# Chunked attention and two feed-forward layers: the first layer's weights stored later as two halves, and SiLU as one ScalarE operation

## The chip, the cores and the metric

The kernel runs on one core of a Trainium2 chip. The metric is the device time of one execution in microseconds (us); where several runs are given, their median. Shorter is better.

## The reference, cut to what matters

Three stages run in a row, all in float32: attention in chunks of 32 queries with 8 memory keys, then two feed-forward layers (FFN) on 3072 tokens of width 512.

```python
attn = softmax(scale * q_c @ k_full.T) @ v_full      # 4 x 8 heads, 768 positions, head size 64
x = relu(attn_tokens @ w_in) ** 2 @ w_out            # first FFN,  512 -> 2048 -> 512
g, val = x @ w_gate, x @ w_val                       # second FFN, 512 -> 1536 -> 512
out = (g * sigmoid(g) * val) @ moe2_w_out
```

The product of g and sigmoid(g) is SiLU. All weights arrive as pairs of 32-bit words (64-bit floats), so each must be put together into float32 before use.

## The kernel before, in words

**Products.** TensorE multiplies in a rounded float32 form. For accuracy each operand is split into a rounded part hi and a rest lo, and a product is three matmuls: lo by hi, hi by lo, hi by hi (`TERMS`, line 41). `split` (line 440) makes the two parts: an ACT copy writes hi, and a subtraction on DVE or POOL writes lo.

**Stages.** The 3072 tokens are six blocks of 512. Attention is 24 units, four to a block. Four units run ahead of all else; the others run beside the matmuls of blocks one to four (numbered j = 0 to 3 in the code). Blocks one to four go through the first FFN directly: for each of 16 groups i of 128 hidden columns, `first_layer` (line 698) is 12 matmuls, `hidden` (713) squares the ReLU and splits it, and `first_out` (728) is 12 matmuls. The second FFN then runs over three pairs of blocks with a product of two-by-two blocks in seven multiplications instead of eight; for the last pair the first FFN goes that way too. In such a pair `quads` (934) computes the hidden columns, `out_layer` (1040) the output, and `second_quads` (1006) gives the element work between the products. The seven-way product needs sums and differences of weight blocks, the left sides. `sides` (758) forms one set of them from two inputs, splits each, and stores it to DRAM through the buffers of pool G4; `Left.load_in` (818) and `Left.load_out` (845) fetch them again.

**Weights.** `words` (382) loads 512 KB of word pairs into a buffer of pool G4, and with two ACT and four DVE operations makes a 128x512 float32 tile `a` in pool G2. `prep1` (685) does this for the 32 pieces of the first FFN (16 of w_in, 16 of w_out) during block one (j = 0): it calls `words`, **stores `a` to DRAM** (lines 689 to 692, tensors `w1d`, shown as win and wout in the trace), and splits `a` into the tile that the matmuls read (`w1b`, 1024 wide: hi, then lo). That tile stays in SBUF until block four is done. Much later the 16 sets of left sides of the first FFN (`left1`, lines 1216 to 1225) read the stored `a` back: `whole_of` (858) loads one 128x512 tile in one part (w_in, 256 KB) or two (w_out, 128 KB each), 48 loads in all, 8.4 MB. The 18 sets of the second FFN (`left2`, lines 1212 to 1215) use `words` instead.

**SiLU.** `third` and `second` in `second_quads` (lines 1015 to 1023) add the last product of g, write sigmoid(g) with ACT into another tile, and multiply that tile by g with `sub` (459) on DVE or POOL, whichever the planner takes. There are two such multiplications for each of 12 groups and three pairs, 72 in all.

**Order.** Nothing is scheduled by hand: `Plan` (86) lists every operation with an assumed cost for each engine that may do it, ranks it by when TensorE needs it, and plays the program through on paper, one event after another. The result is a fixed order for each engine. On the chip each engine, and the DMA queue of SP through which all transfers are issued, takes its instructions in that order and waits at each until its inputs are there. A pool has as many buffers as `sizes` (line 328) says: G4 three and G2 six, and two and four more after the tile of block three's tokens (pool X1) is given up. Each set of left sides has a due time in the plan, taken from `SIDES` (line 305): (start, spacing, number) for the two groups, left2 and left1.

```python
def whole_of(parts):
    ...
            pl.op(
                {"SP": 0.08},
                lambda key=key, src=src, o=o, wide=wide: nc.sync.dma_start(
                    out=at(a)[:, o : o + wide], in_=w1d[key][:, src : src + wide]
                ),
                (w1k[key], token), ((a, n),), move=rate(512 * wide),
            )
```

Of the kernel before, what the change touches and what calls it, by code (L numbers as in the profile page):

```python
# [9 lines left out]
F32 = mybir.dt.float32  # L10
# [3 lines left out]
AF = mybir.ActivationFunctionType  # L14
ALU = mybir.AluOpType
AX = mybir.AxisListType

P = 128
# [8 lines left out]
NF1, NF2 = DFF1 // P, DFF2 // P  # L27
# [274 lines left out]

STAGED = 14.5
FIRST = -9.0
SIDES = ((150.0, 20.5, NF2 + NF2 // 2), (540.0, 18.0, NF1))

BY_PE = tuple(range(8))

# [1 line left out]
C512 = {"ACT": 0.63}  # L310
EITHER = {"ACT": 0.63, "DVE": 0.72}
DIFF = {"DVE": 0.69, "POOL": 1.3}
# [3 lines left out]
def rate(nbytes):  # L316
    return nbytes / 370e3
# [3 lines left out]
def tile_chunked_attention_two_ffn(ctx: ExitStack, tc, qd, kd, vd, w1, w2, wo2, out):  # L321
    nc = tc.nc
    pl = Plan()
# [6 lines left out]
    dr = ctx.enter_context(tc.tile_pool(name="dr", bufs=1, space=bass.MemoryType.DRAM))  # L330
# [35 lines left out]
    def home(b):  # L366
        if b.pool in BEYOND and b.slot >= sizes[b.pool]:
            name, first = BEYOND[b.pool]
            return name, b.slot - sizes[b.pool] + first
        return b.pool, b.slot  # L370

    def at(b):
        name, n = home(b)
        return homes[name][n]

    def external(name):
        return pl.buf(None, name)

    xb = external("x")
# [60 lines left out]
    def split(dst, src, reads, keys, n=512, diff=None):  # L440

        k = n / 512
        pl.op(
            {"ACT": 0.2 + 0.43 * k},
            lambda: nc.scalar.activation(out=dst(HI), in_=src(), func=AF.Copy),  # L445
            reads, [(b, (q, HI)) for b, q in keys],
        )
        costs = {"DVE": 0.16 + 0.56 * k, "POOL": 0.25 + 1.1 * k} if diff is None else diff

        def low(e):  # L450
            eng = nc.gpsimd if e == "POOL" else nc.vector
            eng.tensor_tensor(out=dst(LO), in0=src(), in1=dst(HI).bitcast(F32), op=ALU.subtract)  # L452

        pl.op(
            costs, low, list(reads) + [(b, (q, HI)) for b, q in keys], [(b, (q, LO)) for b, q in keys],
            shared=diff is not FROM,
        )

    def sub(out, x, y, op=ALU.subtract, engs=None):


        def run(e):
            eng = nc.gpsimd if e == "POOL" else nc.vector
            eng.tensor_tensor(out=out[1](), in0=x[1](), in1=y[1](), op=op)  # L464

        return pl.op(engs or DIFF, run, (x[0], y[0]), (out[0],), shared=engs is not FROM)

    def copy(out, x, engs=None, func=AF.Copy):
        def run(e):
            if e == "DVE":  # L470
                nc.vector.tensor_copy(out[1](), x[1]())
            else:
                nc.scalar.activation(out=out[1](), in_=x[1](), func=func)  # L473

        return pl.op(engs or {"ACT": 0.6}, run, (x[0],), (out[0],))

    def whole(b):
        return (b, lambda: at(b))
# [198 lines left out]
    def unit(u, pool="A4"):  # L677
        return Unit(u, pool, pool == "S0")


    w1b = {}
    w1d = {(k, i): dr.tile([P, 512], F32, name=f"w{k}{i}") for k in ("in", "out") for i in range(NF1)}
    w1k = {k: external("w") for k in w1d}

    def prep1(kind, i):
        a = words(w1[i, :, 1024 * (kind == "out") :][:, 0:1024])
        b = pl.buf("W1" if kind == "out" and i >= 4 else "R", "w1")
        w1b[kind, i] = b
        pl.op(
            {"SP": 0.08}, lambda: nc.sync.dma_start(out=w1d[kind, i], in_=at(a)),  # L690
            (a,), (w1k[kind, i],), move=rate(262144),
        )
        split(
            lambda h: at(b)[:, 512 * h : 512 * h + 512], lambda: at(a), (a,), ((b, 0),),
            diff={"DVE": 0.72, "POOL": 1.35},
        )

    def first_layer(i, xb):
        hp, w = pl.buf("PS", "hp"), w1b["in", i]

        def run():
            x = at(xb).rearrange("p (h k t) -> p h k t", h=2, k=KC)
            terms = [(a, b, k) for a, b in TERMS for k in range(KC)]
            for n, (a, b, k) in enumerate(terms):
                nc.tensor.matmul(  # L705
                    at(hp), at(w)[:, 512 * a + k * P : 512 * a + (k + 1) * P], x[:, b, k, :],
                    start=(n == 0), stop=(n == len(terms) - 1),
                )

        pl.op({"PE": 2.75}, run, (xb, w), (hp,), tail=0.2)  # L710
        return hp

    def hidden(hp):
# [41 lines left out]

    due = [a + n * d for a, d, k in SIDES for n in range(k)]

# [100 lines left out]
    def whole_of(parts):  # L858


        def make(token):
            a, o = pl.buf("G2", "a"), 0
            for n, (key, src, wide) in enumerate(parts):
                pl.op(
                    {"SP": 0.08},
                    lambda key=key, src=src, o=o, wide=wide: nc.sync.dma_start(
                        out=at(a)[:, o : o + wide], in_=w1d[key][:, src : src + wide]
                    ),
                    (w1k[key], token), ((a, n),), move=rate(512 * wide),
                )  # L870
                o += wide
            return a

        return make
# [131 lines left out]
    def second_quads(left, r):  # L1006

        got = []

        def begin(n):  # L1010
            a, d, e, f = (pl.buf("T2", x) for x in "adef")
            b, c = pl.buf("U", "b"), pl.buf("U", "c")
            got.append((b, c))

            def third(k):
                sub(whole(e), whole(e), whole(k), ALU.add, FROM)
                copy(whole(f), whole(e), func=AF.Sigmoid, engs=C512)
                sub(whole(f), whole(f), whole(e), ALU.mult)

            def second(k):  # L1020
                sub(whole(a), whole(a), whole(k), ALU.add, FROM)
                copy(whole(d), whole(a), func=AF.Sigmoid, engs=C512)
                sub(whole(d), whole(d), whole(a), ALU.mult)

            def seventh(k):
                sub(whole(c), whole(k), whole(c), ALU.add, FROM)
                sub(whole(c), whole(c), whole(f), ALU.mult)

            return {
                1: lambda k: copy(whole(a), whole(k)),  # L1030
                5: lambda k: copy(whole(c), whole(k)),
                6: lambda k: copy(whole(e), whole(k)),
                3: third, 2: second, 7: seventh,
                4: lambda k: sub(whole(b), whole(k), whole(d), ALU.mult, FROM),
            }

        quads([lambda q=q: left.load_in(q) for q in range(NF2)], r, begin)
        return got
# [65 lines left out]
    def put_out(p):  # L1104
        def put(x, row, col):
# [16 lines left out]
            out=ident, in_=ident, pattern=[[-1, P]], compare_op=ALU.is_equal, fill=0.0,  # L1122
# [6 lines left out]
    xs = {0: pl.buf("X1", "x")}  # L1129
# [44 lines left out]
    for j in range(DIRECT):  # L1174
        if j + 1 < DIRECT:
            xs[j + 1] = pl.buf(("X", "X1")[j % 2], "x")
        for i in range(NF1):
            if j == 0:
                for kind, n in at_slot.get(i, ()):
                    pl.due = FIRST if i == 0 else None  # L1180
                    prep1(kind, n)
                    pl.due = None
                if i == NF1 - 1:
                    for s in (NF1, NF1 + 1):
                        for kind, n in at_slot.get(s, ()):
                            prep1(kind, n)
            for what in "MTLAB":
                for op, u in todo.get((j, i), ()):
                    if op != what:
                        continue  # L1190
                    if op == "A":
                        units[u] = unit(u)
                        units[u].scores()
                    elif op == "B":
                        units[u].weigh()
                    elif op == "T":
                        units[u].turn_pe() if u in BY_PE else units[u].turn()
                    elif op == "M":
                        units[u].mix()
                    elif op == "L":  # L1200
                        if u // 4 < DIRECT:
                            units[u].leave(xs[u // 4], u % 4)
                        else:
                            units[u].leave_far(u // 4 - DIRECT, u % 4)
            hp = first_layer(i, xs[j])
            pend.append((j, i, hidden(hp)))
            if len(pend) > LAG:
                flush()
# [18 lines left out]
    src, token = (*yd[:-1], xd), (*yb[:-1], xb)  # L1227
# [112 lines left out]
```

## Time and profile before

| | |
|---|---|
| median of 3 runs | 1145.23 us (1144.47 to 1146.02) |
| the profiled execution: own time, span | 1146.57 us, 1144.9 us |
| TensorE (PE) busy | 1101.8 us, 96% of the span |
| VectorE (DVE) busy | 901.6 us, 79% |
| ScalarE (ACT) busy | 609.2 us, 53% |
| GpSimd (POOL) busy | 242.2 us, 21% |
| moved by DMA | 305.24 MB, mean 267 GB/s |
| chain that ended last | PE 72%, DVE 11%, DMA 8%, issue 5%, ACT 4%, POOL 1% |

In the trace a tile is named by its pool without its number: g and gg are tiles of G4, f and ff of G2, t of T2, u and a of U, r and x hold operands for TensorE, ps is PSUM. `tma` and `tmb` are left2's sides in DRAM (for the hidden layer and the output), `tla` and `tlb` those of left1. A line can be that of a helper: 452 is the lo part of `split`, 464 the body of `sub`, 473 that of `copy`, 425, 433, 410 and 417 the DVE operations of `words`. "SPq" is the queue in which SP issues transfers. An arrow `<-` in a wait points at what the engine waited for.

The stretches of the span, read off where the lines change: attention ahead of block one to 30 us; block one to about 135; blocks two to four to about 468, with left2's sides beside them; the first pair's hidden layer to 576 and its output to 645; the second pair's to 758 and 824; the first FFN of the last pair to 965; the last pair's second FFN from there to the end.

### The profile page before, as it was taken

What the parts mean: (1) busy time and instruction counts of PE and PEld (TensorE: products, weight loads), DVE (VectorE), ACT (ScalarE), POOL (GpSimd) and SP (SyncE); (2) the same over time, 40 slices, a digit from 0 to 9 for tenths busy, and PEclk for the clock granted to TensorE, in tenths of its full rate; (3) what the DMA queues carried; (4) which work ended last, traced back from release to release, by engine and by line L of the source; (5) the groups of instructions that cost most, each with busy time, mean ns of one, the idle gap of its engine ahead of it and who ended that gap; (6) DMA issues with size and microseconds to landing.
All of it is one profiled execution on the core that took longest, in us unless ns stands there. A gap on an engine that the chain in (4) does not pass through costs nothing.

```text
span 1144.9 us, 17301 instructions
## 1 busy us (share of the span) xinstructions
PE 1101.8 (96%) x6044; PEld 893.9 (78%) x6044; DVE 901.6 (79%) x1573; ACT 609.2 (53%) x1071; POOL 242.2 (21%) x202
## 2 busy tenths in 40 slices
PE   5898999999999999999899999999999999999998
PEld 5676788888888887788687788878888887888786
DVE  6989898869888998789998967898847963645981
ACT  3878764455546566455564444565536642433560
POOL 2211000012121342212944511334500100000100
PEclk9999999999999999999999999999999999999999
DMA  8877855566756877999689999989984677755552
GB/s 340 303 250 260 267 188 179 170 232 227 263 192 243 293 267 282 399 345 357 205 307 360 365 415 371 361 275 335 352 333 148 202 228 275 259 193 175 178 179 94
DMA packets 111591, 305.24 MB, mean 267 GB/s; under 512 B 12048, under 2 KB 20240, under 8 KB 111504
## 3 DMA queue, kind: packets, MB, share of 16 engines
q1 hardware_dynamic: 111504, 304.14, 75.3%
q8 instruction: 48, 0.79, 0.3%
q14 instruction: 39, 0.32, 0.1%
HBM read 218.63 MB, written 85.46 MB: 266 GB/s over the span
## 4 chain that ended last, share of the span: by engine, by line
PE 72%; DVE 11%; DMA 8%; issue 5%; ACT 4%; POOL 1%; SPq 0%; ACTq 0%; DVEq 0%; POOLq 0%
PE ps L926 30%; PE ps L1063 17%; PE ps L705 11%; PE ps L733 10%; DMA g<-in_w 4%; DVE r L452 2%; PE ps L519 2%; PE ps L646 2%; DVE f L425 1%; ACT r L445 1%; DVE t L464 1%; DMA tla<-g 1%; DVE u L464 1%; DMA s<-in_k 1%; DMA r<-tmb 1%
## 5 line engine op out<-in xcount | busy, mean ns | idle before, releaser
L926 PE MATMUL ps<-r,r 128*128 128x512 f32 x1314 | 317.2, 391 | 8.6 <-DVE u L464 5.2
L926 PEld LDWEIGHTS ps<-r,r 128*128 128x128 f32 x1314 | 246.1, 188 | 65.4 <-DVE u L464 6.8
L473 ACT ACTIVATE t<-ps 128x512 f32<-128x512 f32 x171 | 100.9, 595 | 208.1 <-PE ps L926 92.5
L1063 PE MATMUL ps<-r,r 128*128 128x512 f32 x816 | 192.9, 389 | 1.6 <-ACT r L445 1.3
L1063 PEld LDWEIGHTS ps<-r,r 128*128 128x128 f32 x816 | 153.0, 188 | 34.3 <-ACT r L445 1.7
L733 PE MATMUL ps<-r,w 128*128 128x512 f32 x576 | 141.5, 395 | 7.1 <-DVE w L452 6.4
L733 PEld LDWEIGHTS ps<-r,w 128*128 128x128 f32 x576 | 107.4, 188 | 33.3 <-DVE w L452 8.6
L452 DVE TENSOR_TENSOR r<-u,r 128x512 fp32r<-128x512 f32 x138 | 101.3, 755 | 33.5 <-ACT r L445 27.2
L445 ACT ACTIVATE r<-u 128x512 fp32r<-128x512 f32 x149 | 89.0, 625 | 65.3 <-PE ps L1063 29.3
L705 PE MATMUL ps<-xx,r 128*128 128x512 f32 x384 | 98.2, 405 | 5.0 <-DVE r L452 4.7
L705 PE MATMUL ps<-x,r 128*128 128x512 f32 x384 | 94.3, 394 | 0.0
L705 PEld LDWEIGHTS ps<-xx,r 128*128 128x128 f32 x384 | 71.7, 190 | 23.8 <-DVE r L452 6.1
L926 PE MATMUL ps<-r,x 128*128 128x512 f32 x330 | 83.5, 395 | 1.9 <-ACT t L473 1.0
L464 DVE TENSOR_TENSOR t<-t,ps 128x512 f32<-128x512 f32 x72 | 49.0, 682 | 45.8 <-PE ps L926 40.1
L705 PEld LDWEIGHTS ps<-x,r 128*128 128x128 f32 x384 | 70.9, 188 | 15.4
L595 DVE STREAM_TRANSPOSE a<-t 32x128 f32<-32x128 f32 x256 | 77.4, 303 | 5.0 <-PE ps L646 0.9
L473 ACT ACTIVATE t<-t 128x512 f32<-128x512 f32 x72 | 45.3, 631 | 57.5 <-DVE t L464 55.9
L926 PEld LDWEIGHTS ps<-r,x 128*128 128x128 f32 x330 | 62.5, 190 | 16.6 <-DVE r L452 1.6
L452 POOL TENSOR_TENSOR r<-t,r 128x512 fp32r<-128x512 f32 x29 | 40.7, 1404 | 140.3 <-ACT r L445 114.3
L445 ACT ACTIVATE g<-f 128x512 fp32r<-128x512 f32 (+1 forms) x70 | 40.2, 576 | 35.8 <-POOL f L464 11.7
L464 POOL TENSOR_TENSOR u<-u,u 128x512 f32<-128x512 f32 x8 | 11.9, 1494 | 198.5 <-DVE r L452 196.0
L926 PE MATMUL ps<-x,r 128*128 128x512 f32 x180 | 51.4, 394 | 0.5 <-ACT t L473 0.5
(152 smaller groups left out, 1686.5 us busy)
## 6 DMA issues: line engine op xcount, KB each, us to landing
r<-tma SPq DMA_DIRECT2D x88, 512.0 KB, 6.3
r<-tmb SPq DMA_DIRECT2D x56, 512.0 KB, 5.5
g<-in_w SPq DMA_DIRECT2D x54, 512.0 KB, 5.1
tma<-g SPq DMA_DIRECT2D x29, 512.0 KB, 4.6
r<-tlb SPq DMA_DIRECT2D x24, 512.0 KB, 4.4
a<-in_q SPq DMA_DIRECT2D x20, 512.0 KB, 4.4
a<-in_k SPq DMA_DIRECT2D x20, 512.0 KB, 4.9
a<-in_v SPq DMA_DIRECT2D x20, 512.0 KB, 4.5
```

The costliest lines, as they stand in the source:

```text
L425: lambda: nc.vector.scalar_tensor_tensor(out=at(a).bitcast(I32), in0=word(1), scalar=-0x40000000, in1=at(a).bitcast(I32), op0=ALU.bitwise_ ...
L445: lambda: nc.scalar.activation(out=dst(HI), in_=src(), func=AF.Copy),
L452: eng.tensor_tensor(out=dst(LO), in0=src(), in1=dst(HI).bitcast(F32), op=ALU.subtract)
L464: eng.tensor_tensor(out=out[1](), in0=x[1](), in1=y[1](), op=op)
L473: nc.scalar.activation(out=out[1](), in_=x[1](), func=func)
L519: nc.tensor.matmul(o[64 * par : 64 * par + 64, s, f, m, :], q[:, s, m, ci, :], k[:, s, m, ci, :], start=True, stop=True,)
L595: nc.vector.transpose(out=o[g : g + 32, hh, :, :, m, :].rearrange("k s (f c) q -> k s f c q", c=2)[:, :, :, par, :], in_=a[r : r + 32, :, ...
L646: nc.tensor.matmul(o[64 * hh : 64 * hh + 64, 2 * s : 2 * s + 2, CH * ci : CH * ci + CH], a[:, hh, s, ci, :], b[:, hh, s, ci].rearrange("p ...
L705: nc.tensor.matmul(at(hp), at(w)[:, 512 * a + k * P : 512 * a + (k + 1) * P], x[:, b, k, :], start=(n == 0), stop=(n == len(terms) - 1),)
L733: nc.tensor.matmul(at(accs[m]), at(w)[:, 512 * a + m * P : 512 * a + (m + 1) * P], at(h2)[:, 512 * b : 512 * b + 512], start=(i == 0 and n ...
L926: nc.tensor.matmul(at(bank), at(w[slot])[:, o : o + P], at(r[i, n])[:, 512 * b : 512 * b + 512], start=(first and n == 0 and m == 0), stop ...
L1063: nc.tensor.matmul(at(bank[i][n]), at(w[i][g // 2])[:, o : o + P], at(r)[:, 512 * b : 512 * b + 512], start=(first and m == 0), stop=(g == ...
```

## The change

The 32 stores of `a` leave `prep1`. In their place `keep1` stores the finished tile, hi and lo, 512 KB for each piece: the 16 of w_in beside block two (j = 1), the 16 of w_out beside block three (j = 2). The name `begun` orders each store behind the matmuls of group i in the plan alone; no memory stands behind it. `whole_of` loads hi and lo into two tiles of G2 and adds them on DVE or POOL, so 48 loads become 96 and 32 additions come in. The multiplications behind the sigmoid go, and ACT writes SiLU itself. The due times of the left sides move.

```diff
-SIDES = ((150.0, 20.5, NF2 + NF2 // 2), (540.0, 18.0, NF1))
+SIDES = ((150.0, 22.0, NF2 + NF2 // 2), (560.0, 16.0, NF1))
...
-    w1d = {(k, i): dr.tile([P, 512], F32, name=f"w{k}{i}") for k in ("in", "out") for i in range(NF1)}
+    w1d = {(k, i): dr.tile([P, 1024], F32, name=f"w{k}{i}") for k in ("in", "out") for i in range(NF1)}
...
     def prep1(kind, i):
...
-        pl.op(
-            {"SP": 0.08}, lambda: nc.sync.dma_start(out=w1d[kind, i], in_=at(a)),
-            (a,), (w1k[kind, i],), move=rate(262144),
-        )
...
+    def keep1(kind, i, j):
+
+        b = w1b[kind, i]
+        pl.op(
+            {"SP": 0.08},
+            lambda: nc.sync.dma_start(out=w1d[kind, i], in_=at(b).bitcast(F32)),
+            (b, (begun, (j, i))), (w1k[kind, i],), move=rate(524288),
+        )
...
     def whole_of(parts):
...
+                for b, c in ((a, src), (t, 512 + src)):
+                    pl.op(
+                        {"SP": 0.08},
+                        lambda b=b, c=c, key=key, o=o, wide=wide: nc.sync.dma_start(
+                            out=at(b)[:, o : o + wide], in_=w1d[key][:, c : c + wide]
+                        ),
+                        (w1k[key], token), ((b, n),), move=rate(512 * wide),
+                    )
...
+            pl.op(
+                DIFF,
+                lambda e: (nc.gpsimd if e == "POOL" else nc.vector).tensor_tensor(
+                    out=at(a), in0=at(a), in1=at(t), op=ALU.add
+                ),
+                keys, keys[: len(parts)], shared=True,
+            )
...
             def third(k):
                 sub(whole(e), whole(e), whole(k), ALU.add, FROM)
-                copy(whole(f), whole(e), func=AF.Sigmoid, engs=C512)
-                sub(whole(f), whole(f), whole(e), ALU.mult)
+                copy(whole(f), whole(e), func=AF.Silu, engs=C512)
 
             def second(k):
                 sub(whole(a), whole(a), whole(k), ALU.add, FROM)
-                copy(whole(d), whole(a), func=AF.Sigmoid, engs=C512)
-                sub(whole(d), whole(d), whole(a), ALU.mult)
+                copy(whole(d), whole(a), func=AF.Silu, engs=C512)
...
+            hp = first_layer(j, i, xs[j])
+            if j in (1, 2):
+                keep1(("in", "out")[j - 1], i, j)
```

## Rows read from the trace of the kernel before

**Rows 1.** Windows by stage: us, busy (instructions) of PE, PEld, DVE, ACT, POOL; PEclk, DMA share, GB/s
```profile
30.00:135.00 105.00, 91.60 (x570) 70.36 (x569) 95.49 (x170) 81.95 (x145) 18.42 (x15) 0.98 0.81 271
135.00:400.00 265.00, 265.00 (x1954) 214.35 (x1953) 222.36 (x522) 143.26 (x250) 41.58 (x40) 1.00 0.65 223
...
468.00:545.00 77.00, 76.25 (x335) 62.90 (x336) 65.62 (x103) 40.78 (x72) 19.82 (x15) 1.00 0.97 360
545.00:576.00 31.00, 25.42 (x98) 19.75 (x98) 30.41 (x31) 15.87 (x30) 27.27 (x21) 0.89 0.65 224
576.00:645.00 69.00, 66.43 (x288) 53.52 (x287) 61.80 (x95) 39.93 (x74) 29.87 (x21) 1.00 0.92 331
645.00:758.00 113.00, 110.65 (x484) 90.33 (x484) 90.57 (x133) 57.24 (x104) 34.57 (x33) 1.00 1.01 379
758.00:824.00 66.00, 65.87 (x289) 53.92 (x289) 60.24 (x91) 36.41 (x68) 28.28 (x21) 1.00 0.91 316
```

**Rows 2.** Waits of PE in block one, 30 to 135 us: total us, times, longest
```profile
PE ps L733 <- DVE w L452: 6.4, 5, 1.5
PE ps L705 <- DVE r L452: 4.7, 5, 1.9
```

**Rows 3.** Waits of SP's queue in the same stretch: total us, times, longest
```profile
SPq L386 <- DVE f L425: 43.1, 25, 4.6
SPq L690 <- DVE f L417: 14.0, 13, 1.9
```

**Rows 4.** DMA issues, 30 to 135 us: count, KB each, median us to landing
```profile
g<-in_w SPq DMA_DIRECT2D x27, 512.0 KB, 5.3
```

**Rows 5.** DMA issues, 135 to 320 us
```profile
g<-in_w SPq DMA_DIRECT2D x14, 512.0 KB, 4.8
...
a<-in_q SPq DMA_DIRECT2D x11, 512.0 KB, 4.4
```

**Rows 6.** Waits of PE, 545 to 645 us
```profile
PE ps L926 <- DVE u L464: 4.6, 2, 3.4
```

**Rows 7.** Groups by line and shape, whole span: count, busy us, mean ns, idle before
```profile
L464 DVE TENSOR_TENSOR t<-t,t 128x512 f32<-128x512 f32 x61 | 46.4, 764 | 1.6 <-ACT t L473 1.6
...
L473 ACT ACTIVATE t<-t 128x512 f32<-128x512 f32 x72 | 45.3, 631 | 57.5 <-DVE t L464 55.9 <-DVE a L464 0.6
...
L464 POOL TENSOR_TENSOR t<-t,t 128x512 f32<-128x512 f32 x11 | 15.1, 1370 | 111.7 <-ACT t L473 111.6
```

**Rows 8.** The same view, ACT alone: the table load at the first sigmoid
```profile
L473 ACT ACT_TABLE_LOAD x1 | 1.3, 1283 | 0.0
```

**Rows 9.** Groups by line and shape, 440 to 580 us
```profile
L464 POOL TENSOR_TENSOR t<-t,t 128x512 f32<-128x512 f32 x10 | 13.8, 1377 | 63.6 <-ACT t L473 63.5
L464 DVE TENSOR_TENSOR t<-t,t 128x512 f32<-128x512 f32 x14 | 11.1, 799 | 0.0
```

**Rows 10.** Timeline of DVE, 541 to 548 us: start, us, operation
```profile
541.56 0.68 DVE L452 TENSOR_TENSOR gg<-ff,gg 128x512 fp32r<-128x512 f32 x1
542.16 1.78 DVE L464 TENSOR_TENSOR u<-u,t 128x512 f32<-128x512 f32 x1
```

**Rows 11.** Timeline of POOL, the same stretch
```profile
542.10 1.30 POOL L452 TENSOR_TENSOR r<-u,r 128x512 fp32r<-128x512 f32 x1 [3.29 <-ACT r L445]
```

**Rows 12.** Timeline, 525 to 600 us: the last word pairs of left2
```profile
537.67 0.42 SPq L386 DMA_DIRECT2D g<-in_wo  x1
```

**Rows 13.** Chain that ended last, at the ends of two hidden layers: start, us, what
```profile
744.23 2.01 DVE t L464 x2
...
1082.07 1.92 DVE t L464 x2
```

**Rows 14.** Windows of 50 us: the one with the most GB/s
```profile
650.00:700.00 50.00, 49.22 (x216) 40.09 (x215) 35.95 (x55) 22.72 (x40) 9.71 (x11) 1.00 1.03 404
```

**Rows 15.** DMA issues, 560 to 824 us
```profile
f<-wout SPq DMA_DIRECT2D x22, 128.0 KB, 5.9
f<-win SPq DMA_DIRECT2D x9, 256.0 KB, 7.1
```

More of the change, by code (lines that the diff above doesn't have):

```diff
@@ L696, in prep1, with first_layer @@
         )
-    def first_layer(i, xb):
+    def keep1(kind, i, j):
[5 more added lines that the diff above has]
+        )
+    begun = external("begun")
+    def first_layer(j, i, xb):
         hp, w = pl.buf("PS", "hp"), w1b["in", i]
@@ L708, in run @@
                 )
-        pl.op({"PE": 2.75}, run, (xb, w), (hp,), tail=0.2)
+        pl.op({"PE": 2.75}, run, (xb, w), (hp, (begun, (j, i))), tail=0.2)
         return hp
@@ L861, in make @@
         def make(token):
-            a, o = pl.buf("G2", "a"), 0
+            a, t, o = pl.buf("G2", "a"), pl.buf("G2", "t"), 0
             for n, (key, src, wide) in enumerate(parts):
[L864 to L870, printed above, removed]
-                o += wide
+                for b, c in ((a, src), (t, 512 + src)):
[6 more added lines that the diff above has]
+                    )
+                o += wide
+            keys = [(b, n) for b in (a, t) for n in range(len(parts))]
+            pl.op(
[5 more added lines that the diff above has]
+            )
             return a
@@ L1204, in tile_chunked_attention_two_ffn @@
                             units[u].leave_far(u // 4 - DIRECT, u % 4)
-            hp = first_layer(i, xs[j])
+            hp = first_layer(j, i, xs[j])
+            if j in (1, 2):
+                keep1(("in", "out")[j - 1], i, j)
             pend.append((j, i, hidden(hp)))
```

## The prediction

> **What bounds the kernel now.** I read the windows by stage first, for where TensorE (PE) is not busy. In blocks two to four it never stops: 265.00 of 265 us, at full granted clock [rows 1]. Nothing that the change does there can gain, and it costs nothing as long as that cover stands. Time is lost in two places. In block one PE is busy 91.60 of 105 us, so 13.4 us are idle. At the end of the first pair's hidden layer it is busy 25.42 of 31 us, and the mean granted clock is 0.89 of full there [rows 1]: 5.6 us idle, and 0.11 x 31 = 3.4 us to the lower clock. The output layer behind it is short of 2.6 us, and the second pair's hidden layer of 2.4 us. Ahead of block one lies attention, and the change has no part in it.
>
> Then the waits, for whose fault it is. In block one PE waits for the lo parts of weights (6.4 us) and of hidden tiles (4.7 us), both DVE's [rows 2]. DVE is busy 95.49 of 105 us [rows 1]. The queue of SP shows the other half of the loop: the loads of word pairs wait 43.1 us, in 25 waits, for line 425, the last operation that reads a G4 buffer [rows 3]. So block one is a ring of three buffers: load, two ACT and three DVE operations, next load. With 27 loads in 105 us [rows 4], one turn of a buffer takes 3 x 105 / 27 = 11.7 us, of which 5.3 us is the load's time to landing. Ring and DVE are nearly equal bounds.
>
> At 545 to 576 us PE waits for DVE's sums over tiles u (4.6 us) [rows 6], DVE is busy 30.41 and POOL 27.27 of 31 us [rows 1]. POOL is no free help: the same size of DVE operation takes 0.68 us alone and 1.78 us when it starts 0.06 us behind a POOL operation of 1.30 us [rows 10, 11].
>
> **The change, part by part.** The sum is made against the profiled execution's 1146.57 us (span 1144.9 us); the median shown is 1145.23, that is 1.34 us less, so I take the sum off the median in the end.
>
> *The 32 stores leave block one.* That is 8.4 MB fewer transfers in a stretch that moved 271 GB/s at a DMA share of 0.81; they also leave SP's queue, where they waited for DVE (14.0 us on line 417 alone) [rows 1, 3] with loads behind them. That wait cost little, since those loads had to wait for line 425 anyway. What the stores cost is landing time of the loads. Later, at a share of 0.65, the same loads land in 4.8 us and attention's loads of equal size in 4.4 [rows 1, 5]. So a turn shrinks by 0.5 to 0.9 us of 11.7: 4 to 8 us over 105. DVE caps it: with 95.49 us of work it can give back 9.5 us at most, and it becomes the next wait. I take 4 us, the low end, because DVE is already 91% busy. Bounds: 0 (DVE takes all of it) to 9.5.
>
> *Stores of hi and lo in blocks two and three.* 32 x 0.52 = 16.8 MB more, beside PE that never waits. On SP they are 32 issues at about 0.42 us [rows 12], an estimate of 13 us of queue time over 175 us; they wait for nothing, since hi and lo are long made. Behind them stand loads of word pairs for left2. If these land as in block one, 0.5 us later [rows 4, 5], left2's sides slip by some us; their last load was issued at 537.67 us [rows 12], the output layer that needs them begins at 576. I cost it at nothing. If that cover went, PE would wait at 576 for what is missing, at most a few us.
>
> *SiLU in ACT.* Each of the 72 ACT operations stays, at 631 ns [rows 7]; no row has a SiLU, so its price lies between that and 631 + 764 ns, as if ACT did both steps one after the other; I take 631, the row of the same operation on the same tiles, and ACT, idle for half of 545 to 576 us, could carry the other end as well. One table load of 1283 ns stands at the first sigmoid [rows 8], and one will stand at the first SiLU. The 72 multiplications go: 46.4 us of DVE and 15.1 of POOL [rows 7]. What this is worth is read where DVE was late. From 440 to 580 us 14 of them were on DVE (11.1 us) and 10 on POOL (13.8 us) [rows 9], and each POOL operation can hold a DVE operation up by some 1.1 us [rows 10]. That is some 20 us of DVE's time in a stretch where PE lost 5.6 + 3.4 = 9.0 us. Also left1's first set moves from 540 to 560, out of this stretch. I take 8 of the 9 us. Bounds: 0 to 11.6, which adds the 2.6 us behind 576.
>
> At the ends of the other hidden layers two multiplications stand in the chain, 2.01 and 1.92 us [rows 13]. Without them the chain falls back on what stands beside it, so I take half, 2 us for both. Bounds 0 to 4.
>
> *32 additions for left1, between 560 and 824 us.* At the price of the like operation, 764 ns on DVE or 1370 on POOL [rows 7], they are 24 us of DVE. The second pair's 24 multiplications (18 us) leave the same stretch, so the balance there is near nothing; but in 576 to 645 us about 8 additions (6.1 us) come to a DVE that is busy 61.80 of 69 and lose nothing there. DVE has 7.2 us free. I take a loss of 1 us, bounds 0 to 6.
>
> *8.4 MB more to read there,* and one set of sides (2.4 MB) that moved in: 10.8 MB. The room: up to the best 50 us, 404 GB/s [rows 14], the three stretches from 576 to 824 [rows 1] have 73 x 69 + 25 x 113 + 88 x 66 us = 13.7 MB. Up to 379 GB/s, the mean of the longest full stretch, they have 7.5 MB. So between 0 and 3.3 MB / 379 GB/s = 8.7 us are uncovered. I take 2, nearer 404, since the queue that starts PE's loads runs ahead of PE. 48 more issues on SP (about 20 us of 248) stay beside other work.
>
> Sum: -4 - 8 - 2 + 1 + 2 = **-11 us**: 1135.6 for the profiled execution, 1134.2 for the median.
>
> **A rule against it.** The trace shows 379 GB/s held for 113 us and 404 for 50 [rows 1, 14]. The Trainium skill, "DMA: Bandwidth & Descriptors" (section "Where 436 GB/s comes from"), says that the HBM side limits a core to about 358 GB/s, and elsewhere ties that figure to both cores of a pair streaming; here one runs. By that figure 576 to 824 us would have no more than 2.3 MB of room, 8.5 MB would be late, some 24 us at 358 GB/s, and the change would end near 1156. The rows of this case pass the figure already, so it gets 0.01 of the chances.
>
> **The rivals.**
> 1. *Block one is DVE's, not the ring's.* For it: 95.49 of 105 us. Against: 43.1 us of waits for buffers. Block one then gains nothing: 1145.2 - 7 = 1138.
> 2. *The DMA ceiling is 379, not 404.* 8.7 us uncovered in place of 2: 1141. For it: the share is 1.01 in the second pair's hidden layer [rows 1]. Against: PE lost only 0.8 us in the 50 us at 404 GB/s [rows 14].
> 3. *Slower: the additions block DVE's queue.* An addition needs two or four loads and stands first in its set. The plan believes in 3.0 us and 0.7 us of moving; left1's loads took 7.1 and 5.9 us to land [rows 15]. In DVE's fixed order whatever stands behind the addition waits, PE's sums too. Sixteen sets x 3.4 us is 54 us of standing still if every set's addition is placed at once and on DVE; DVE has 248 - 212.6 = 35 us free from 576 to 824 [rows 1], so 19 us reach PE. With the gains of 4, 8 and 2 and the DMA's 2 that is 1145.2 - 12 + 19 = 1152. It decides once more than about 47 us of the 54 come true. Against: the plan ranks sets of sides low, so most operations stand well behind their loads, and part will go to POOL.
> 4. *SiLU sits in another table than what runs beside it.* Then table loads of 1283 ns [rows 8] come back between SiLU and the absolute values of `words`; six sets remain beside the first pair, two loads for each of 12 tiles, 31 us of ACT, which is idle 15 of 31 us where it hurts. Half of it reaching PE is 15 us: 1149. Sigmoid and those absolute values ran side by side until after 537.67 us [rows 12] with the one load of [rows 8], which speaks against it.
>
> **How the numbers follow.** The forecast's case gets 0.52, rival 1 0.16, rival 2 0.14, rival 3 0.12, rival 4 0.03; 0.03 is left for a new order of the plan that no row shows, and the figure above. A measurement of this kernel tells about 0.2%, 2.3 us, from no change. The forecast's case and rival 1 are faster; rival 2 (about -4) is faster in most of its spread and the same in the rest; rivals 3 and 4 are slower. That gives faster 0.74, same 0.09, slower 0.17. The low end of the range is all gains at their bounds, 9.5 + 9 + 4 = 22.5: 1122.7. The high end takes in most of rival 3, 1151. The forecast's case alone would be 1126 to 1140.
>
> **What would show it.** Right: between 30 and 135 us PE idles under 10 us, the loads of word pairs land in under 5 us; from 545 to 576 the granted clock is near 1 and the wait of line 926 for sums over u is gone; no multiplication t<-t,t is left; one table load beside the first. Wrong: the waits for lo parts in block one stay at 11 us (rival 1); DMA share over 1.0 all through 576 to 824 with PE waiting for r<-tma or r<-tmb (rival 2); DVE waiting for f<-win or f<-wout (rival 3); more than two table loads (rival 4).

## The result and the profile after

The changed kernel takes 1134.6 us (median of 4 runs, 1134.11 to 1135.41) where the kernel before takes 1145.62 on the same chips: a ratio of 0.9902, 95% interval 0.9884 to 0.9919, so 11 us less. The profiled execution of after took 1134.11 us, its span 1132.4 (before: 1146.57 and 1144.9).

First the windows by stage of the kernel after, in the stretches of [rows 1] and with the same columns. The stages come up to 12 us sooner now, so a stretch no longer begins quite where its stage does.

```profile
30.00:135.00 105.00, 97.10 (x623) 74.27 (x623) 101.39 (x180) 84.76 (x151) 23.74 (x15) 1.00 0.65 218
135.00:400.00 265.00, 265.00 (x1954) 214.72 (x1953) 224.94 (x511) 141.08 (x249) 55.11 (x51) 1.00 0.82 283
...
468.00:545.00 77.00, 77.00 (x341) 63.77 (x340) 58.59 (x101) 42.98 (x76) 5.82 (x6) 1.00 0.97 349
545.00:576.00 31.00, 28.67 (x118) 22.93 (x117) 30.90 (x42) 18.35 (x34) 13.44 (x9) 0.94 0.73 260
576.00:645.00 69.00, 67.63 (x298) 55.65 (x298) 67.90 (x98) 36.51 (x66) 25.48 (x20) 1.00 1.00 373
645.00:758.00 113.00, 108.46 (x473) 89.11 (x472) 86.74 (x136) 55.97 (x102) 19.32 (x13) 0.98 0.99 371
758.00:824.00 66.00, 66.00 (x293) 54.67 (x292) 61.51 (x99) 40.11 (x74) 20.94 (x10) 1.00 1.00 366
```

Read against [rows 1], line by line: in block one (30 to 135) PE is busy 97.1 us in place of 91.6, DVE 101.4 in place of 95.5, and the DMA share fell from 0.81 to 0.65. In 135 to 400 the share rose from 0.65 to 0.82, where the stores went, and PE is still busy all the time. At 545 to 576 PE's idle time fell from 5.6 to 2.3 us and the granted clock rose from 0.89 to 0.94. In the second pair's hidden layer (645 to 758) it is the other way round: 2.4 us idle became 4.5.

Next PE's waits in block one, which answer to [rows 2], and the loads of word pairs there, which answer to [rows 4].

```profile
PE ps L740 <- DVE w L452: 2.7, 2, 1.4
PE ps L712 <- DVE r L452: 2.5, 3, 1.6
```
```profile
g<-in_w SPq DMA_DIRECT2D x29, 512.0 KB, 4.4
```

The two waits of 11.1 us together are down to 5.2, and a load lands in 4.4 us in place of 5.3. Last the rows of SiLU, in the groups by line and shape; they answer to [rows 7] and [rows 8].

```profile
L473 ACT ACTIVATE t<-t 128x512 f32<-128x512 f32 x72 | 45.5, 632 | 63.0 <-DVE t L464 60.3 <-DVE u L464 1.7
...
L397 ACT ACT_TABLE_LOAD x1 | 1.3, 1283 | 0.8 <-PEq L1343 0.8
L473 ACT ACT_TABLE_LOAD x1 | 1.3, 1283 | 0.0
```

SiLU takes 632 ns where the sigmoid took 631, there are two table loads as before, and no group t<-t,t is left on DVE or POOL behind it.

One sign that the prediction had named did not come: line 926's wait for DVE's sums over u (line 942 in the kernel after) is not gone, and the granted clock from 545 to 576 us is 0.94, not near 1. From 530 to 640 us PE still waits, in place of the row of [rows 6] and 3.4 us for other operations:

```profile
PE ps L942 <- DVE u L464: 3.7, 3, 2.0
```

**Where the time came from.** Three points in the program, read from the last start of a line and from the chain, tell it: the last matmul of block four starts at 446.6 us (before 452.1), the run of 282 output matmuls of the last pair's first FFN at 881.89 (893.33), the last matmul at 1128.3 (1140.7). So 5.5 us were won by the end of block four, 5.9 between there and 882, and 1.0 behind it. That is 12.4 us between these two executions; the medians differ by 11. The 5.9 us lie in one stage: the last matmul of the first pair's hidden layer starts at 567.4 us (578.7), and from there to the 282 matmuls both kernels take the same time, 314.5 and 314.6 us.

### The profile page after: what moved, and what is told of

It is laid out like the page before. It is cut to its first block, busy times and chain, and to the rows that moved or that the text cites. A ratio compares the mean times of both kernels' runs of the same rounds, so it can differ in the third digit from the quotient of the medians.

```text
span 1132.4 us, 17301 instructions
## 1 busy us (share of the span) xinstructions
PE 1097.3 (97%) x6044; PEld 893.7 (79%) x6044; DVE 891.4 (79%) x1576; ACT 611.8 (54%) x1077; POOL 200.6 (18%) x157
## 4 chain that ended last, share of the span: by engine, by line
PE 80%; DVE 9%; DMA 5%; ACT 3%; issue 2%; POOL 1%; SPq 0%; DVEq 0%; ACTq 0%; POOLq 0%
PE ps L942 34%; PE ps L1077 18%; PE ps L712 13%; PE ps L740 12%; PE ps L519 2%; PE ps L646 2%; DVE r L452 2%; DVE f L425 1%; DVE f L433 1%; DVE f L410 1%; DMA s<-in_k 1%; ACT r L445 1%; DMA tla<-g 1%; DMA u<-yd 1%; DVE u L464 1%
## 5 line engine op out<-in xcount | busy, mean ns | idle before, releaser
L473 ACT ACTIVATE t<-ps 128x512 f32<-128x512 f32 x172 | 101.4, 594 | 191.3 <-PE ps L942 79.3
L740 PE MATMUL ps<-r,w 128*128 128x512 f32 x564 | 138.6, 396 | 2.8 <-DVE w L452 2.7
L445 ACT ACTIVATE r<-u 128x512 fp32r<-128x512 f32 x144 | 85.6, 624 | 40.3 <-PE ps L1077 16.6
L452 DVE TENSOR_TENSOR r<-u,r 128x512 fp32r<-128x512 f32 x130 | 90.7, 716 | 17.0 <-ACT r L445 12.4
L712 PE MATMUL ps<-x,r 128*128 128x512 f32 x384 | 94.3, 394 | 0.0
L445 ACT ACTIVATE r<-a 128x512 fp32r<-128x512 f32 x63 | 39.1, 626 | 53.0 <-PE ps L1077 27.1
L452 POOL TENSOR_TENSOR r<-t,r 128x512 fp32r<-128x512 f32 x30 | 45.7, 1522 | 109.3 <-ACT r L445 91.2
L942 PE MATMUL ps<-x,r 128*128 128x512 f32 x231 | 62.3, 391 | 0.2 <-DVE x L452 0.2
L942 PE MATMUL ps<-r,x 128*128 128x512 f32 x243 | 61.0, 392 | 0.0
L452 POOL TENSOR_TENSOR r<-u,r 128x512 fp32r<-128x512 f32 x14 | 21.4, 1528 | 222.6 <-ACT r L445 222.6
L445 ACT ACTIVATE g<-f 128x512 fp32r<-128x512 f32 (+1 forms) x75 | 42.8, 574 | 25.1 <-DVE f L433 8.8
```

The source lines that it names most:

```text
L712: nc.tensor.matmul(at(hp), at(w)[:, 512 * a + k * P : 512 * a + (k + 1) * P], x[:, b, k, :], start=(n == 0), stop=(n == len(terms) - 1),)
L740: nc.tensor.matmul(at(accs[m]), at(w)[:, 512 * a + m * P : 512 * a + (m + 1) * P], at(h2)[:, 512 * b : 512 * b + 512], start=(i == 0 and n ...
L942: nc.tensor.matmul(at(bank), at(w[slot])[:, o : o + P], at(r[i, n])[:, 512 * b : 512 * b + 512], start=(first and n == 0 and m == 0), stop ...
```

## The experiments

Each kernel was timed in three rounds beside the kernel before. Ratios are to the kernel before on the same chip, with 95% intervals; its own medians there were 1143.8 to 1145.6 us. A median is of four executions (of ten for the due times alone and the two kernels with other stores); within one kernel they lie 1.3 to 7.3 us apart.

| kernel | median us | ratio | interval |
|---|---|---|---|
| the change | 1134.6 | 0.9902 | 0.9884 to 0.9919 |
| SiLU alone | 1134.5 | 0.9910 | 0.9884 to 0.9936 |
| stores and additions alone | 1135.7 | 0.9915 | 0.9890 to 0.9940 |
| due times alone | 1143.7 | 0.9993 | 0.9979 to 1.0007 |
| the change, old due times | 1127.6 | 0.9849 | 0.9827 to 0.9871 |
| the change, 32 other stores in block one | 1139.3 | 0.9957 | 0.9940 to 0.9974 |
| the change, 32 old stores in block one | 1141.5 | 0.9979 | 0.9968 to 0.9990 |
| the change without additions | 1126.2 | 0.9845 | 0.9831 to 0.9860 |
| the change without second loads | 1128.7 | 0.9871 | 0.9851 to 0.9891 |
| the change, left2's due times new, left1's old | 1135.1 | 0.9932 | 0.9905 to 0.9959 |
| the change, left1's due times new, left2's old | 1128.3 | 0.9866 | 0.9851 to 0.9882 |
| the change, left1 due 1 us later | 1125.3 | 0.9842 | 0.9823 to 0.9861 |
| sums beside blocks two and three | 1134.8 | 0.9917 | 0.9900 to 0.9933 |

### The parts one by one

**SiLU alone:** the kernel before with this edit, in `third` and likewise in `second`:

```diff
-                copy(whole(f), whole(e), func=AF.Sigmoid, engs=C512)
-                sub(whole(f), whole(f), whole(e), ALU.mult)
+                copy(whole(f), whole(e), func=AF.Silu, engs=C512)
```

> The kernel before with SiLU alone; stores, loads and due times as they were. Theory (two separate gains: block one's buffer ring, and DVE's queue at the end of the first pair): block one stays as it was, last first-layer matmul of block four within 1 us of 442.9 us, and the end of the first pair's hidden layer, 576 us, comes 6 to 9 us sooner; time 1136 to 1139 us. Rival A (the due times made the gain at the first pair): 576 moves by under 2 us, time 1143 to 1146. Rival B (what is won there is lost again before the second output layer, where left1's sets still crowd DVE): 576 comes sooner, but the end by under 3 us, 1143.

Measured 0.9910, at 1134.5 us a little better than the theory's 1136 to 1139. The first output matmul comes at 567.0 us in place of 576.2, just beyond the theory's 6 to 9 us; of these 9 us, 2.6 were there already in block four (440.3 against 442.9), more than the 1 us allowed. That point misleads, though: with due times alone, below, it comes at 566.5, ahead of a wait of 5.2 us. The last matmul of the first pair's hidden layer, counted from the last one of block four, tells more: it starts 121.3 us later here, 126.6 before and 124.8 with due times alone. Even these 5 us are not shown to be SiLU's own: the next kernel, which keeps the sigmoid, has 119.4. Rival A falls, for the due times were old; so does rival B, for nothing was lost again.

**Stores and additions alone:** the change, with sigmoid, its multiplications and `SIDES` put back as before.

```diff
-SIDES = ((150.0, 22.0, NF2 + NF2 // 2), (560.0, 16.0, NF1))
+SIDES = ((150.0, 20.5, NF2 + NF2 // 2), (540.0, 18.0, NF1))
...
-                copy(whole(f), whole(e), func=AF.Silu, engs=C512)
+                copy(whole(f), whole(e), func=AF.Sigmoid, engs=C512)
+                sub(whole(f), whole(f), whole(e), ALU.mult)
```

> The kernel before with the stores moved, two loads and an addition in place of one load; sigmoid, its multiplications and the old due times stay. Theory: block one gains 5 to 7 us (last first-layer matmul of block four near 436), and 32 additions on a DVE that still has the multiplications give 2 to 6 of it back: 1140 to 1143. Rival (the additions wait for late loads at the head of DVE's queue): DVE stands 10 us or more on f<-win and f<-wout, time 1146 to 1152. Rival (block one is bound by DVE and gained only with the plan's new order): 442.9 moves by under 2 us.

Measured 0.9915, better than the theory's 1140 to 1143. Block one did as expected (435.5), but the additions gave nothing back: from the last matmul of block four to the last of all this kernel takes 684.5 us, the kernel before 688.7, though DVE carries both the multiplications and the additions. DVE waited for no load of the stored weights between 560 and 824 us.

**Due times alone:**

```diff
-SIDES = ((150.0, 20.5, NF2 + NF2 // 2), (540.0, 18.0, NF1))
+SIDES = ((150.0, 22.0, NF2 + NF2 // 2), (560.0, 16.0, NF1))
```

> The kernel before with the new due times alone. Theory: they are no cause, 1144 to 1148 us, the stretch 545 to 576 keeps its 5 us of idle PE. Rival A (moving left1's first set from 540 to 560 is what cleared that stretch): idle there under 2 us and the time 1137 to 1140.

Measured 0.9993: no difference that can be told. The wait for DVE's sums at the end of the first pair's hidden layer is still there, as this row of PE's waits from 530 to 640 us shows, the counterpart of [rows 6]:

```profile
PE ps L926 <- DVE u L464: 6.9, 3, 5.2
```

So moving left1's first set out of the stretch does not clear it; with SiLU alone that wait is 1.5 us:

```profile
PE ps L926 <- DVE u L464: 1.5, 1, 1.5
```

**The change with old due times:** `SIDES` alone put back.

> The changed kernel with the old due times. Theory: 1133 to 1138, stores and SiLU do nearly all. Rival A: 1139 to 1143, and PE idles 4 us or more around the end of the first pair's hidden layer.

Measured 0.9849, and neither theory had that: the new due times made the change 6 us worse, though by themselves they do nothing. This was the open question of the last runs.

At the old due times four kernels make a square: 1 before, 0.9910 with SiLU, 0.9915 with stores and additions, 0.9849 with both. SiLU gains 0.0090 alone and 0.0066 beside the stores, some 10 and 8 us; the stores gain 0.0085 alone and 0.0061 beside SiLU, some 10 and 7. Each corner is one order of the plan, though, and the last runs show what an order is worth.

### What the stores cost in block one

Both kernels are the change with 32 more stores of 256 KB in `prep1`, to a tensor that nobody reads. The first stores the hi half of the finished tile, so no buffer of G2 waits for it; the second stores `a`, as before the change.

```diff
+        pl.op(
+            {"SP": 0.08},
+            lambda: nc.sync.dma_start(out=w1s[kind, i], in_=at(b)[:, 0:512].bitcast(F32)),
+            ((b, (0, HI)),), ((w1k[kind, i], 1),), move=rate(262144),
+        )
```

> The changed kernel with 32 more stores in block one, of the hi half of each finished weight tile (256 KB each) to a tensor that nobody reads: traffic and SP issues as before the change, but no buffer of G2 is held by them. Theory (the loads' landing time in the ring of G4 buffers): block one gives back most of its gain, the last first-layer matmul of block four at 440 to 443 us instead of 436, loads of word pairs land in 5.2 to 5.5 us instead of 4.4, time 1138 to 1141. Rival (holding the tile a in G2 until its store has landed was the cost): block one keeps its gain, 435 to 437, time 1134 to 1136.

```diff
+        pl.op(
+            {"SP": 0.08}, lambda: nc.sync.dma_start(out=w1s[kind, i], in_=at(a)),
+            (a,), ((w1k[kind, i], 1),), move=rate(262144),
+        )
```

> The changed kernel with the 32 old stores of a back in block one, to a tensor that nobody reads: traffic, SP issues and G2 buffers held, as before the change. Theory (landing): the same as with the hi half stored, within 1.5 us, 1138 to 1141. Rival (holding): 1139 to 1142 here and 1135 there.

Of the kernel with the hi halves: the window of block one, its loads of word pairs there, and its first-layer matmuls of the blocks in pool X (shortest, median and longest ns; first and last start).

```profile
30.00:135.00 105.00, 92.25 (x572) 71.15 (x572) 95.69 (x169) 81.83 (x144) 21.13 (x16) 0.98 0.81 269
```
```profile
g<-in_w SPq DMA_DIRECT2D x28, 512.0 KB, 5.3
```
```profile
L718 PE MATMUL ps<-x,r x384: 387/389/501, 136.3 to 441.5; 128*128 128x512 f32 x192
```

And the first two of the kernel that stores `a`:

```profile
30.00:135.00 105.00, 91.69 (x590) 70.41 (x592) 96.67 (x172) 82.56 (x145) 18.75 (x15) 1.00 0.84 274
```
```profile
g<-in_w SPq DMA_DIRECT2D x28, 512.0 KB, 5.2
```

Stores that hold no G2 buffer bring back everything of [rows 1] and [rows 4] for block one: PE at 92 us, landing at 5.3 us, the last first-layer matmul of block four at 441.5 us. So the held buffer is not needed for the loss. One rival is left: these stores also stand in SP's queue, ahead of loads, until their data are made, as this kernel's queue shows from 30 to 135 us:

```profile
SPq L696 <- ACT r L445: 26.7, 17, 4.0
SPq L696 <- ACT w L445: 15.7, 9, 3.0
SPq L386 <- DVE f L425: 15.6, 16, 3.1
```

The traces settle it load by load. For the 5th to the 32nd load of word pairs I read when line 425 freed the buffer, when line 386 issued the next load into it, and when that load had landed (means, us):

| | freed to issued | issued to landed | landed to freed again | whole turn |
|---|---|---|---|---|
| before | 0.16 | 5.19 | 6.01 | 11.36 |
| the change | 0.10 | 4.37 | 6.07 | 10.54 |
| with 32 stores of the hi half | 0.19 | 5.30 | 5.78 | 11.26 |
| with 32 old stores | 0.16 | 5.19 | 5.87 | 11.23 |

The queue costs a load 0.2 us at most in the mean. Between before and the change the turn shrinks by 0.82 us, and the landing time by 0.82. So it is the landing time in the ring of G4 buffers. Storing `a` itself gives the same within block one (440.9), and in the end 2.3 us more, where the theory allowed 1.5; the two intervals overlap, and if there is a difference, it could be the buffer or the order of the plan.

### What the additions and second loads cost

**Without additions:**

```diff
-            pl.op(
-                DIFF,
-                lambda e: (nc.gpsimd if e == "POOL" else nc.vector).tensor_tensor(
-                    out=at(a), in0=at(a), in1=at(t), op=ALU.add
-                ),
-                keys, keys[: len(parts)], shared=True,
-            )
```

> The changed kernel without the 32 additions: hi and lo are loaded both, but left1's sides are formed from hi alone (the last pair's first FFN loses the lo part of its weights). Theory: the additions are what PE waits for at the end of the second pair's hidden layer (4.5 us in the profile after): that wait falls under 2 us, the time by 2 to 5 us, 1130 to 1133. Rival (the second reads are the cost): within 1 us of 1134.6.

**Without second loads:** one load in place of two, and the addition adds hi to itself. The second G2 tile of each load goes with it.

```diff
-                for b, c in ((a, src), (t, 512 + src)):
+                for b, c in ((a, src),):
...
-                    out=at(a), in0=at(a), in1=at(t), op=ALU.add
+                    out=at(a), in0=at(a), in1=at(a), op=ALU.add
```

> The changed kernel without the second loads: the 32 additions stay and add hi to itself (left1's sides are then those of twice the weights' hi part; results of the last pair differ), 8.4 MB less are read. Theory: additions and not traffic cost time, so within 1.5 us of 1134.6. Rival (DMA at its ceiling from 576 to 824): 1128 to 1132, with DMA share under 0.95 there.

Both are faster than the change: 0.9845 and 0.9871 to its 0.9902, 7 and 4 us, the second with intervals that overlap a little. The first gained more than the theory's 2 to 5 us; at the end of the second pair's hidden layer PE waits 1.3 us, under 2 as the theory said. The second falls to the rival by its time though not by its traffic: the DMA share is 0.99 from 576 to 824 us, and the wait at that end is gone here too, with every addition in place. Taken at their word, additions and second loads would each be most of the cost. But the change with old due times keeps all additions and loads and is as fast as these two. Together with the next runs this makes it likely that both merely left an unlucky order.

In the chain of the kernel after one sees that order's cost, the last 8 us ahead of PE's restart at 744.25 us:

```profile
736.30 1.78 DVE u L464
738.09 1.70 DVE g L452
739.79 0.60 DVE a L464
740.39 1.07 DVE g L452
741.46 0.60 DVE t L464
742.06 0.60 DVE ff L883
742.66 0.60 DVE t L464
743.26 0.34 DVE f L464
743.59 0.61 DVE a L464
744.21 0.04 issue
744.25 2.93 PE ps L942 x6
```

Lines with g, f and ff belong to a set of left1 (883 is an addition, 0.60 us); they stand in DVE's queue among the sums over t and a that PE waits for. The three at 736.30, 738.09 and 740.39 take 4.6 us in place of about 1.8, and POOL is busy beside them without a break from 734.40 to 740.91; the sum at 739.79, which reads PSUM, takes 0.60 there. PE's wait, from the same kernel, and operations of POOL ahead of it:

```profile
PE ps L942 <- DVE a L464: 4.5, 1, 4.5
```
```profile
725.14 3.22 POOL L464 TENSOR_TENSOR u<-u,u 128x512 f32<-128x512 f32 x1 [4.83 <-DMA f<-wout]
...
735.79 1.75 POOL L883 TENSOR_TENSOR f<-f,ff 128x512 f32<-128x512 f32 x1
737.49 1.74 POOL L452 TENSOR_TENSOR r<-u,r 128x512 fp32r<-128x512 f32 x1
739.20 1.71 POOL L452 TENSOR_TENSOR x<-u,x 128x512 fp32r<-128x512 f32 x1
```

POOL itself had stood 4.8 us, until 725.14, for a load of a stored weight. Whether that pushed its later work into these us is not shown; the kernel with 561, below, has POOL standing 10.2 us for such loads between 560 and 824 us and does not lose time here.

### Due times or order

Four last kernels: the change with one half of the due times new and the other old, with left1's start 1 us later, and with the additions moved.

```diff
-SIDES = ((150.0, 22.0, NF2 + NF2 // 2), (560.0, 16.0, NF1))
+SIDES = ((150.0, 22.0, NF2 + NF2 // 2), (540.0, 18.0, NF1))
```

> The changed kernel, left1's due times back at (540, 18), left2's spacing new (22). With all due times old it ran at 0.985 of before, with all new at 0.990. Theory (left1's sets, 16 us apart from 560 on, crowd DVE at the end of the second pair's hidden layer): 0.984 to 0.986 here, and no wait over 2 us there. Rival (left2's wider spacing is the cost): 0.989 to 0.991. Rival (neither is a cause, one order of the plan is unlucky): anything, and not in line with the kernel that has the other half.

```diff
-SIDES = ((150.0, 22.0, NF2 + NF2 // 2), (560.0, 16.0, NF1))
+SIDES = ((150.0, 20.5, NF2 + NF2 // 2), (560.0, 16.0, NF1))
```

> The changed kernel, left2's spacing back at 20.5, left1's due times new (560, 16). Theory (left1's crowding): 0.989 to 0.991, with the wait of 4 us for a sum over a tile of U at the end of the second pair's hidden layer. Rival (left2's spacing): 0.984 to 0.986.

```diff
-SIDES = ((150.0, 22.0, NF2 + NF2 // 2), (560.0, 16.0, NF1))
+SIDES = ((150.0, 22.0, NF2 + NF2 // 2), (561.0, 16.0, NF1))
```

> The changed kernel with left1's first due time 1 us later (561 in place of 560), which no cause named so far should feel. Theory (left1's crowding): within 1.5 us of the changed kernel, 0.989 to 0.992. Rival (one unlucky order of the plan): over 3 us off it, most likely 0.984 to 0.987.

A shift of one start by 1 us takes 0.9902 to 0.9842, intervals apart. Left1's new times with left2's old ones give 0.9866, between the two ranges, and no wait of 4 us: the longest at that end is 1.2. Left2's new times alone give 0.9932 with no wait at that end at all, so left1's crowding is out. Within their intervals these two would still allow left2's wider spacing as the cost; but the kernel with 561 has that spacing too and is the fastest of all. What is left is the order which the plan happens to find. PE's waits from 440 us on follow it: in the five kernels at 0.9902, 0.9932, 0.9849, 0.9866 and 0.9842 they come to 10.7, 9.4, 7.0, 5.6 and 5.5 us, in executions of 1134.1, 1132.7, 1128.5, 1127.3 and 1124.6 us; the 9.4 us of the second are spread over several waits of at most 2.2. Windows of the second pair's hidden layer, first of the kernel after, then of the one with 561, show the same stage with and without the wait:

```profile
636.00:747.00 111.00, 105.26 (x457) 86.45 (x458) 85.55 (x133) 54.84 (x99) 20.88 (x15) 0.99 0.99 372
```
```profile
635.00:740.00 105.00, 104.70 (x462) 86.11 (x461) 78.66 (x123) 51.16 (x92) 22.11 (x20) 1.00 1.02 384
```

**Sums beside blocks two and three:** old due times; `keep1` adds hi and lo into a tile of G2 and stores 256 KB, with a due time of its own, and `whole_of` is that of before.

```diff
+        pl.due = 140.0 + 98.0 * (j - 1) + 6.0 * i
+        b, s = w1b[kind, i], pl.buf("G2", "s")
+        pl.op(
+            DIFF,
+            lambda e: (nc.gpsimd if e == "POOL" else nc.vector).tensor_tensor(
+                out=at(s), in0=at(b)[:, 0:512].bitcast(F32), in1=at(b)[:, 512:1024].bitcast(F32),
+                op=ALU.add,
+            ),
+            (b, (begun, (j, i))), (s,), shared=True,
+        )
```

> Old due times, SiLU, and the sum of hi and lo formed beside blocks two and three instead (32 additions there, then one store of 256 KB each; left1 loads 256 KB per tile as before the change). Blocks two to four have PE busy all through and DVE at 84%, so the additions should be hidden there; from 560 to 824 us 32 additions and 8.4 MB of reads are gone. Theory (additions and second reads still cost something at old due times): 0.981 to 0.984, 1123 to 1126 us. Rival (at old due times they are hidden): 0.984 to 0.986. Rival (the additions delay left2's sides in blocks two and three, and the output layer of the first pair waits): 0.987 or more.

Measured 0.9917, in the worst of the three ranges, but not for its reason: from 440 us on PE waits for no load of left2's sides. It is also within the spread of orders just seen, so whether the additions are better placed there stays open.

**What stands out of that spread.** The last start of a first-layer matmul tells block one's share; the time from block four's last matmul to the last product of a hidden layer, or to the last matmul of all, tells the rest. They are read from the first and last start of those lines in each profile, so from one execution of each kernel.

| | with stores in block one (5 kernels) | without (9 kernels) |
|---|---|---|
| last first-layer matmul, us | 440.3 to 442.9, mean 441.3 | 435.2 to 436.9, mean 436.0 |

| | sigmoid (before, due times alone, stores alone) | SiLU, additions and second loads as in the change (7 kernels) |
|---|---|---|
| block four to last hidden product, us | 629.6 to 633.8, mean 631.2 | 618.7 to 627.8, mean 623.3 |
| block four to last matmul, us | 684.5 to 688.7, mean 686.1 | 674.9 to 684.0, mean 679.5 |

By the first table the groups are 5.3 us apart in the mean and do not come near each other: that is the stores. In the second the row to the last hidden product flatters SiLU: the kernels with sigmoid run 12 output matmuls ahead of the last six hidden ones, those with SiLU only six, and have 1.4 us more to go. To the last matmul the means are 6.6 us apart, for SiLU with all that comes with it, but the groups only 0.5, less than executions of one kernel differ; with the square above this makes a gain likely and leaves its size open. By the same measures SiLU alone, with no addition, has 623.1 and 679.3, the change without additions 620.3 and 676.5, without second loads 621.5 and 677.7: all inside the range of those that have them, so the additions and second loads cost nothing that can be told from the order. The five orders of the change itself (old due times, the two halves, 1 us later, and the change) span 0.9842 to 0.9932, with a mean of 0.988.

## Why the prediction was right

The sum of -11 us was right, and by thirds of the span too: forecast -4, -6 and -1 for block one, the middle, and the last pair, measured -5.5, -5.9 and -1.0. In the middle that is partly luck: -8 for the first pair and +2 for the rest were forecast, and -5.8 and nothing came. The terms fared differently.

- **Stores out of block one, -4, bounds 0 to 9.5: right in its mechanism, a little low.** Landing fell by 0.8 to 0.9 us, the upper of the two values weighed, and a turn by as much. The last of the 32 pieces freed its buffer 8.0 us sooner (134.6 us, before 142.6), the full price of the turns; 5.3 us of it came through block four. The caution over DVE was right in kind: DVE is now busy 101.39 of 105 us, and PE still waits 5.2 us for its lo parts. Rival 1 (nothing to be had, DVE bound) is out: 32 stores that nobody needs, put back, took PE from 97 to 92 us and the landing time back to 5.3.
- **Stores beside blocks two and three at nothing: right.** PE is busy 265.00 of 265 us again, at a DMA share of 0.82.
- **SiLU at the sigmoid's price: right,** 632 ns to 631, and rival 4 is out, with one table load at SiLU.
- **The end of the first pair, -8: too much there.** Idle time and clock cost 2.3 us and 0.06 x 31 = 1.9 us in the window of after, in place of 9.0: some 5 us. The wait for sums over u, which was to go, is 3.7 us in place of 4.6; most of what went are waits for other operations and the clock. That left1's first set moved out was counted as help; the run with due times alone shows none in its time. The output layer, where +1 was expected, lost 1.4 us in place of 2.6. That SiLU cleared this end by itself is not shown: the kernel with stores and additions alone gets through that hidden layer as fast with the sigmoid, in another order.
- **The ends of the other hidden layers, -2: wrong for the second pair.** A new wait of 4.5 us stands there, in which additions take part, as in rival 3, though not for the reason that it gave: no load was late for DVE, only for POOL. It belongs to one order, and is gone when a due time moves by 1 us.
- **Additions +1 and DMA +2: not seen.** PE waited for no weight tile, though the share was 0.99 to 1.00 from 576 to 824 us. Rival 2 had the ceiling at 379 GB/s; the kernel with 561 moved 384 GB/s for 105 us with PE busy 104.70 of them. The 358 GB/s that the Trainium skill gives in "DMA: Bandwidth & Descriptors" (section "Where 436 GB/s comes from") is passed here too, by 7%; that page ties it to two cores streaming, and one runs.

One slip in the range changed nothing: its low end takes 9 us for the first pair where the bound of that term was 11.6, so all gains at their bounds would be 1120.1 and not 1122.7.

What the prediction did not have was the size of the plan's own scatter. It set aside 0.03 for "a new order of the plan that no row shows". Five orders of the same operations lie 10 us apart, nearly as much as the change is worth, and the due times, to which it gave no term of their own, moved the time by 6 us in the changed kernel and by nothing in the kernel before. The range of 1122.7 to 1151.0 holds all five. That the forecast was hit to the us is luck: the mean of the five orders, 0.988, is a gain of some 14 us, and the change's own order is one of the slower ones.

## What to carry to other kernels

Where loads circulate through few buffers, price a transfer beside them by what it adds to their landing time, times the turns: 0.82 us over 28/3 turns is 7.7 us, and the ring ended 8.0 us sooner. Moving it to a stretch where the busiest engine never waits cost nothing here. Where a program plans its own order, try a few neighbouring settings that should not matter before a few us are put down to an edit: here a shift of 1 us was worth 0.6%, 7 us. The worth of work that leaves an in-order engine is read from the stage where a matmul waits for that engine, and not from its busy time over the span: 61.5 us of multiplications left DVE and POOL here, for some 8 to 10 us of time.

## What the runs showed that was not expected

DMA at a share of 1.0 over 250 us, with 8.4 MB more to read, held PE up nowhere in the kernel after: from 440 us on no wait of PE is for a load (with SiLU alone there is one, of 2.4 us). And DVE took 20 us of additions (28 at 0.68 to 0.77 us; 4 went to POOL at 1.6 to 1.8) in stages where it was 87% busy (216 of 248 us from 576 to 824) without a loss that stands out of the 10 us between orders. Three of the rows of additions, by shape:

```profile
L883 DVE TENSOR_TENSOR f<-f,f 128x512 f32<-128x512 f32 x12 | 9.2, 771 | 0.0
...
L883 DVE TENSOR_TENSOR f<-f,ff 128x512 f32<-128x512 f32 x8 | 5.4, 681 | 0.0
...
L883 POOL TENSOR_TENSOR f<-f,f 128x512 f32<-128x512 f32 x2 | 3.6, 1786 | 12.6 <-DMA out<-ff 12.6
```
